# Splitting one feed-forward block of three tiles into one of one tile and one of two

## The chip, the cores and the metric

The kernel runs on one core of a Trainium2 chip. The metric is the device time of one execution in microseconds. TensorE (PE) does the matrix products and transposes, its weight loads (PEld) overlap them; VectorE (DVE) selects the largest scores, ScalarE (ACT) does activations and copies out of PSUM, GpSimd (POOL) does small element-wise work, and SyncE (SP) issues the transfers.

## The reference

Top-32 attention over 8 batches, 8 heads, 576 queries and keys, head dimension 64, followed by a feed-forward layer with an ELU on the 4608 rows that come out. Everything is float32; the weights arrive as float64.

```
scores = scale * np.matmul(q, k.transpose(0, 1, 3, 2))
kth = np.partition(scores, -top_k, axis=-1)[..., -top_k:-top_k + 1]
mask = scores >= kth
scores = np.where(mask, scores, -1000000000.0)
scores = scores - np.max(scores, axis=-1, keepdims=True)
attn = np.exp(scores)
attn = attn / (np.sum(attn, axis=-1, keepdims=True) + 1e-09)
return np.matmul(attn, v).astype(np.float32)
...
x = np.ascontiguousarray(attn_out.transpose(0, 2, 1, 3)).reshape(B * S, H * D)
...
h = x @ w_in
g = np.where(h > 0.0, h, alpha * (np.exp(np.minimum(h, 0.0)) - 1.0))
return (g @ w_out).astype(np.float32)
```

## The kernel before

**Tiles and steps.** A batch's 576 queries are four tiles of 128 and one tile of the last 64 (`J` = 4 names that one). A step is one tile and one pair of heads; the 64 remaining queries take four heads at once, so they need two steps where a full tile needs four. A batch has 18 steps, the kernel 144, numbered through: batch b starts at step 18 b. In even batches the order is tiles 0 and 1, then 2 and 3, then the remainder; in odd batches the remainder comes first (line 606). So the remainders of an even batch and of the odd one behind it are neighbours: steps 52 and 53 of batch 2, 54 and 55 of batch 3.

**One turn of the loop.** The loop of line 681 writes out the order of all four compute engines by hand; each engine runs its own list in that order. Turn n issues, from the top: the scores of step n+2 on PE (L329) and their copies out of PSUM on ACT (L337); the attention products of a finished group (L448) with their copy into `xT` (L475); the selection of step n on DVE, four rounds of `max` (L349, L363) with `match_replace` (L356) between them; the mask of step n-1 on ACT (L385, L386) with a difference on POOL (L384); the transposes of step n-2 on PE (L422) and their copies into `et` on ACT (L423); and the normalising of step n-1 on POOL (L396 to L403). For batches 1 to 7 DVE also transposes k and q of a coming head pair (L283), some turns ahead of the batch; the keys lie in five buffers, so the second head pair of a coming batch takes the buffer that the first pair of the present batch gives back after its last scores.

**Feed-forward blocks.** Rows of x are gathered in blocks. A block of one, two or three tiles becomes ready when the last attention product of its tiles is copied. It then gives 16 hidden pieces and 4 projection pieces for each of its tiles (lines 565 to 575). A hidden piece (L523) is four float32 products of w_in against all columns of the block: 128 columns for one tile, 256 for two, 384 for three. In the trace each product is two MATMUL records and two weight loads, so a hidden piece is 8 records. Behind it ACT takes the relu twice, the exponential and a copy (L533 to L542), for 4, 2 or 2 hidden pieces together, and POOL adds the gate (L493). A projection piece (L551) is four products of 512 columns, again 8 records, and the last of a tile is copied out and stored (L560, L563).

**The pacing.** Pieces are not issued as soon as they could be. `feed` (line 639) runs four times in a turn and spreads them. It knows for each block a ready time in steps and the work of all blocks before it (`due`, lines 618 to 620), in costs of its own: 1.1, 1.85 and 2.7 for a hidden piece of one, two and three tiles, 3.55 for a projection piece. It releases work at the highest constant rate at which the queue does not run empty before any later block's ready time:

```
        ahead = [(w - fed["sum"]) / (x - fed["at"]) for x, w in due if x > fed["at"]]
        if ahead:
            fed["over"] += max(0.0, share * min(ahead))
```

What is left in the queue when the turns are over runs at the end (line 714). The first pair of batches has seven blocks, the other three pairs four each: tiles 0 and 1; tiles 2 and 3; the remainder of both batches together with tiles 0 and 1 of the odd batch; tiles 2 and 3 of the odd batch (line 585).

Of the kernel before, what the change touches and what calls it, by code (L numbers as in the profile page):

```python
# [80 lines left out]
def kernel(  # L81
# [498 lines left out]
    for b in range(B):  # L580
        if b % 2 == 0:
            rest = 2 * J
            division = [(0,), (1,), (2,), (3,), (rest,), (4, 5), (6, 7)]
            if b > 0:
                division = [(0, 1), (2, 3), (rest, 4, 5), (6, 7)]
            slots = {}
            for part in division:
                blk = Block(len(blocks), len(part))
                blocks.append(blk)
                slots.update((x, (blk, s)) for s, x in enumerate(part))  # L590
        first[b] = len(steps)
        tiles = []
        for qt in range(J + 1):
            r0 = b * S + (JP if qt == J else qt if b == 0 else qt * P)
            if qt == J:
                (blk, slot), c0, n = slots[rest], (b % 2) * R, R
                rows = slice(r0, r0 + R)
            else:
                (blk, slot), c0, n = slots[(b % 2) * J + qt], 0, P
                rows = slice(r0, r0 + J * (P - 1) + 1, J) if b == 0 else slice(r0, r0 + P)  # L600
            c0 += slot * P
            t = Tile(b, qt, rows, blk, slice(c0, c0 + n))
            blk.left += NHP
            blk.tiles[slot].append(t)
            tiles.append(t)
        order = [(0, 1), (2, 3), (J,)] if b % 2 == 0 else [(J,), (0, 1), (2, 3)]
        if b == 0:
            order[:2] = [(0,), (1,), (2,), (3,)]
        for qts in order:
            for hp in range(NHP // 2 if qts == (J,) else NHP):  # L610
                group = Group([tiles[qt] for qt in qts], hp)
                steps += [Step(tiles[qt], hp, group, i) for i, qt in enumerate(qts)]
            for qt in qts:
                n = len(steps)
                tiles[qt].block.ready = n + 2.0 if n <= tight else n + 2.5
# [64 lines left out]
    main, rest, other = slice(0, J), slice(J, J + 1), slice(J + 1, 2 * J + 1)  # L680
# [69 lines left out]
```

## Time and profile before

| what | value |
|---|---|
| device time, median of 3 runs | 1633.7 us (1631.86 to 1633.74) |
| profiled execution: device time, span of its instructions | 1633.17 us, 1631.4 us |
| busy: PE, PEld | 1569.5 us (96%), 1004.7 us (62%) |
| busy: DVE, ACT, POOL | 1454.4 us (89%), 1174.6 us (72%), 711.6 us (44%) |
| hidden products L523 | 2432 records, 542.9 us |
| projection products L551 | 1152 records, 522.5 us |
| DVE's MAX8 L363 | 864, mean 751 ns |
| mean granted TensorE clock | 0.988 |
| transfers | 56.17 MB, mean 34 GB/s |

Busy times of PE are unions of records whose ends are modelled, so a stretch in which PE is "busy" may still hold short waits; the distance from one record's start to the next is the better price of a piece. DVE's last instruction for the selection lies more than 100 us before the end of the span: the end is feed-forward work on PE alone.

### The profile page before, as it was taken

What the parts mean: (1) busy time and instruction counts of PE and PEld (TensorE: products, weight loads), DVE (VectorE), ACT (ScalarE), POOL (GpSimd) and SP (SyncE); (2) the same over time, 40 slices, a digit from 0 to 9 for tenths busy, and PEclk for the clock granted to TensorE, in tenths of its full rate; (3) what the DMA queues carried; (4) which work ended last, traced back from release to release, by engine and by line L of the source; (5) the groups of instructions that cost most, each with busy time, mean ns of one, the idle gap of its engine ahead of it and who ended that gap; (6) DMA issues with size and microseconds to landing.
All of it is one profiled execution on the core that took longest, in us unless ns stands there. A gap on an engine that the chain in (4) does not pass through costs nothing.

```text
span 1631.4 us, 25301 instructions
## 1 busy us (share of the span) xinstructions
PE 1569.5 (96%) x8276; PEld 1004.7 (62%) x8276; DVE 1454.4 (89%) x2980; ACT 1174.6 (72%) x2369; POOL 711.6 (44%) x1535
## 2 busy tenths in 40 slices
PE   4789999999999999999999999999999999999999
PEld 2477666766665757555566666655557575755564
DVE  7899999999999999999999699999999599998000
ACT  6987777877776868778577786868668695958521
POOL 4983345444443444444344443535435353534300
PEclk9779999999999999999999999999999999999999
DMA  8521310012100310022000200012100201000000
GB/s 243 187 79 36 65 37 1 7 22 45 43 1 19 54 37 7 7 40 46 23 8 15 55 21 25 1 28 45 36 14 1 43 1 36 1 13 1 7 14 13
DMA packets 188035, 56.17 MB, mean 34 GB/s; under 512 B 178176, under 2 KB 179200, under 8 KB 187904
## 3 DMA queue, kind: packets, MB, share of 16 engines
q1 hardware_dynamic: 186704, 54.26, 14.1%
q8 instruction: 66, 1.08, 0.3%
q14 instruction: 65, 0.53, 0.1%
q10 hardware_dynamic: 1200, 0.30, 0.1%
HBM read 45.09 MB, written 9.44 MB: 33 GB/s over the span
## 4 chain that ended last, share of the span: by engine, by line
PE 74%; ACT 14%; DVE 5%; POOL 3%; issue 1%; SPq 1%; DMA 1%; ACTq 0%; DVEq 0%; POOLq 0%
PE ops L551 29%; PE hps L523 22%; PE avps L448 10%; PE scps L329 7%; PE eps L422 5%; ACT sc L386 3%; DVE wk L356 2%; ACT sc L385 2%; ACT et L423 2%; DVE m L363 2%; ACT n L542 1%; ACT n L533 1%; ACT n L538 1%; ACT gT L536 1%; POOL sc L403 1%
## 5 line engine op out<-in xcount | busy, mean ns | idle before, releaser
L363 DVE MAX8 m<-wk 128x8 f32<-128x576 f32 x864 | 611.2, 751 | 0.3 <-POOL den L384 0.3
L523 PE MATMUL hps<-xT,w_in 128*128 128x256 f32 (+2 forms) x2432 | 542.9, 373 | 0.0
L551 PE MATMUL ops<-w_out,gT 128*128 128x512 f32 x1152 | 522.5, 598 | 0.0
L523 PEld LDWEIGHTS hps<-xT,w_in 128*128 128x128 f32 x2432 | 404.9, 192 | 97.4 <-issue 25.4
L356 DVE MATCH_REPLACE8 wk<-m,wk 128x576 f32<-128x576 f32 x576 | 424.5, 747 | 0.0
L551 PEld LDWEIGHTS ops<-w_out,gT 128*128 128x128 f32 x1152 | 208.6, 190 | 231.7 <-issue 230.6
L396 POOL TENSOR_SCALAR dene<-den 128x2 f32<-128x2 f32 x144 | 32.5, 225 | 693.1 <-ACT sc L386 692.5
L386 ACT ACTIVATE sc<-sc,den 128x576 f32<-128x576 f32 x288 | 223.4, 776 | 66.1 <-POOL den L384 44.4
L385 ACT ACTIVATE sc<-sc,m 128x576 f32<-128x576 f32 x288 | 225.0, 781 | 9.6 <-DVE m L363 9.5
L337 ACT ACTIVATE sc<-scps 128x576 f32<-128x576 f32 x288 | 170.9, 646 | 77.8 <-PE scps L329 77.8
L448 PE MATMUL avps<-et,vT 128*64 128x256 f32 (+2 forms) x2080 | 205.6, 328 | 20.1 <-ACT et L423 19.7
L329 PE MATMUL scps<-kqT 64*128 64x288 f32 (+1 forms) x1280 | 199.9, 443 | 25.1 <-ACT kqT L305 12.6
L349 DVE MAX8 m<-sc 128x8 f32<-128x576 f32 x288 | 202.6, 747 | 20.6 <-ACT sc L337 20.6
L403 POOL TENSOR_SCALAR sc<-sc,rec 128x576 f32<-128x576 f32 x288 | 213.5, 751 | 14.9
L423 ACT COPY et<-eps 128x512 f32<-128x512 f32 x288 | 164.6, 571 | 66.2 <-PE eps L422 66.2
L356 DVE MATCH_REPLACE8 wk<-m,sc 128x576 f32<-128x576 f32 x288 | 212.2, 746 | 0.0
L448 PEld LDWEIGHTS avps<-et,vT 128*64 128x64 f32 x2080 | 128.0, 141 | 101.0 <-ACT et L423 34.2
L422 PEld LDWEIGHTS eps<-ident,sc 128*128 128x128 f32 x1152 | 143.4, 143 | 72.4 <-issue 53.9
L493 POOL TENSOR_TENSOR gT<-n,gT 128x512 f32<-128x512 f32 (+1 forms) x120 | 166.2, 1385 | 38.0 <-ACT n L542 38.0
L422 PE MATMUL eps<-ident,sc 128*128 128x128 f32 x1152 | 174.1, 277 | 0.1
L329 PEld LDWEIGHTS scps<-kqT 64*128 64x128 f32 (+1 forms) x1280 | 107.0, 182 | 102.5 <-issue 46.2
L533 ACT ACTIVATE n<-hps 128x512 f32<-128x512 f32 (+1 forms) x156 | 87.0, 558 | 58.0 <-PE hps L523 57.1
(45 smaller groups left out, 988.5 us busy)
## 6 DMA issues: line engine op xcount, KB each, us to landing
raw<-in_moe_w_in_dram SPq DMA_DIRECT2D x16, 512.0 KB, 4.9
vT<-in_v_dram SPq DMA_DIRECT2D x64, 128.0 KB, 2.4
raw<-in_moe_w_out_dram SPq DMA_DIRECT2D x16, 512.0 KB, 3.8
out_dram<-osb SPq DMA_DIRECT2D x32, 256.0 KB, 2.0
kin<-in_k_dram SPq DMA_DIRECT2D x112, 72.0 KB, 2.4
qin<-in_q_dram SPq DMA_DIRECT2D x112, 72.0 KB, 2.5
kin<-in_k_dram SPq DMA_DIRECT2D x8, 128.0 KB, 4.7
vT<-in_v_dram SPq DMA_DIRECT2D x64, 16.0 KB, 2.2
```

The source lines that it names most:

```text
L329: nc.tensor.matmul(wide[i][rows, half, 0:HS], kq[part, q0 : q0 + u.t.ql], kq[part, k0 : k0 + HS], start=True, stop=True,)
L349: nc.vector.max(found[i], cur[i])
L356: nc.vector.match_replace(wk[i], found[i], cur[i], TAKEN)
L363: nc.vector.max(found[i], cur[i])
L385: nc.scalar.activation(sc, sc, AF.Prelu, scale=-1.0, bias=low, alpha=1.0 / STEEP)
L386: nc.scalar.activation(sc, sc, AF.Exp, scale=-STEEP, bias=gap, accum_out=u.den[:, i : i + 1])
L403: nc.gpsimd.tensor_scalar(u.sc[:, i, :], u.sc[:, i, :], rec[:, i : i + 1], 1.0, ALU.mult, ALU.mult)
L422: nc.tensor.transpose(ps[:, c * P : (c + 1) * P], sc[:, c0 : c0 + P], ident[:])
L423: nc.scalar.copy(g.et[:, chunks, u.at, :], ps[:, 0 : n * P].rearrange("p (c q) -> p c q", c=n),)
L448: nc.tensor.matmul(ps[i * D : (i + 1) * D, cols], vt[:, 2 * J + i if c == J else i * J + c, :], w, start=(c == 0), stop=(c == J),)
L523: nc.tensor.matmul(blk.h[:, f % bank, :], w_in[:, i, f * P : (f + 1) * P], blk.xT[:, i, 0:n_tok], start=(i == 0), stop=(i == NC - 1),)
L551: nc.tensor.matmul(blk.o[:], blk.gT[f // NG][:, f % NG, s * P : (s + 1) * P], w_out[:, f, :], start=(f == 0), stop=(f == NF - 1),)
```

## The change

In the second pair of batches (b == 2) the block of three tiles, the remainder with tiles 0 and 1 of batch 3, becomes a block of one tile (the remainder of both batches) and, behind it, a block of two (tiles 0 and 1 of batch 3). The third and fourth pairs keep four blocks, the first its seven. The first two blocks of the pair, written again in the diff, stay what they were.

```
         if b % 2 == 0:
             rest = 2 * J
             division = [(0,), (1,), (2,), (3,), (rest,), (4, 5), (6, 7)]
-            if b > 0:
+            if b == 2:
+                division = [(0, 1), (2, 3), (rest,), (4, 5), (6, 7)]
+            elif b > 2:
                 division = [(0, 1), (2, 3), (rest, 4, 5), (6, 7)]
```

The block's ready time, its hidden pieces and its column range follow from the division by the lines above, and `due` has one entry more, so `feed` paces other turns differently too. There are 16 hidden pieces more in the program, 2560 records of L523 where there were 2432; projections, attention and transfers of input keep their number.

## The prediction

> **What bounds the kernel now.** I read the strip of 40 slices first, then the chain of waits by engine.
>
> ```profile
> PE   4789999999999999999999999999999999999999
> DVE  7899999999999999999999699999999599998000
> ...
> PE 74%; ACT 14%; DVE 5%; POOL 3%; issue 1%; SPq 1%; DMA 1%; ACTq 0%; DVEq 0%; POOLq 0%
> ```
>
> Two engines are full at once, and DVE stops in the last slices while PE goes on. So the end is set by PE: its total work, plus every moment in which it waits. Less work or fewer waits on PE shorten the kernel; DVE matters only where it makes PE wait.
>
> Where does PE wait? I cut the span into stretches of equal attention work: turns 30 to 65, 66 to 101 and 102 to 137. Each is 36 turns and has the same step types in the same order. A turn begins on PE with its scores; counting the L329 records in PE's timeline puts turns 30, 66, 102 and 138 at 329.78, 698.09, 1078.49 and 1457.92 us. The stretch view gives, per stretch, its length and then PE, PEld, DVE, ACT and POOL busy with record counts; below it the same for L523 alone, then L551 alone.
>
> ```profile
> 329.78:698.09 368.31, 360.03 (x1893) 232.57 (x1892) 365.64 (x753) 273.67 (x551) 161.93 (x374) 1.00 0.13 26
> 698.09:1078.49 380.40, 378.79 (x1926) 235.61 (x1925) 363.85 (x750) 282.43 (x570) 164.94 (x372) 1.00 0.13 26
> 1078.49:1457.92 379.43, 378.12 (x1926) 235.01 (x1925) 358.14 (x737) 281.88 (x569) 164.99 (x373) 1.00 0.10 22
> ...
> 329.78:698.09 368.31, 121.05 (x512) 93.22 (x512) 1.00 0.13 26
> 698.09:1078.49 380.40, 134.28 (x512) 93.32 (x512) 1.00 0.13 26
> ...
> 329.78:698.09 368.31, 116.75 (x257) 46.34 (x256) 1.00 0.13 26
> 698.09:1078.49 380.40, 131.31 (x288) 51.83 (x288) 1.00 0.13 26
> ```
>
> The first stretch has 32 projection records fewer than the second, and its 512 hidden records are all of 256 columns, while 128 in the second are of 384. Yet it is only 12 us shorter. The prices come from PE's timeline, as distances from the start of a group to the start of the next:
>
> ```profile
> 254.71 2.94 PE L523 MATMUL hps<-xT,w_in 128*128 128x128 f32 x24
> 257.50 0.60 PE L422 MATMUL eps<-ident,sc 128*128 128x128 f32 x4
> ...
> 458.36 3.72 PE L523 MATMUL hps<-xT,w_in 128*128 128x256 f32 x16
> 461.91 0.60 PE L422 MATMUL eps<-ident,sc 128*128 128x128 f32 x4
> ...
> 1486.14 8.01 PE L523 MATMUL hps<-xT,w_in 128*128 128x384 f32 x24
> 1493.99 0.60 PE L422 MATMUL eps<-ident,sc 128*128 128x128 f32 x4
> ```
>
> Eight records to a piece: one tile 2.79/3 = 0.93 us, two tiles 3.55/2 = 1.78 (a lone piece, 447.44 to 449.17, took 1.73; I use 1.75), three tiles 7.85/3 = 2.62 (lone: 2.58; I use 2.60). A projection piece is 3.43 us (8 records from 492.24 to 495.68).
>
> So the second stretch holds 4 projections more (13.7 us) and 16 hidden pieces of three tiles for 16 of two (16 x 0.85 = 13.6 us). At its pace the first would take 380.4 - 27.3 = 353.1 us. It took 368.3: 15.2 us are lost to waiting. The waits of PE in the first two stretches name the place:
>
> ```profile
> PE avps L448 <- ACT et L423: 6.4, 9, 2.4
> ...
> PE avps L448 <- ACT et L423: 1.1, 1, 1.1
> ...
> 454.70 3.72 PE L448 MATMUL avps<-et,vT 128*64 128x256 f32 x18 [2.44 <-ACT et L423]
> ```
>
> Attention products wait for ACT's copies of the transposes, nine times against once. Those copies stand behind the masks in ACT's list, and the masks behind DVE's selection. DVE takes 9.64 us for a turn without a key transpose (first MAX8 of one turn to that of the next, 305.10 to 314.74), nearly 10 with them; PE with 6.5 us of pieces by the planner's costs is a little quicker and runs into DVE's results. The listed waits are 6.4 of the 15.2 us; the rest is in PE records that the view counts as busy, and in a slower clock: behind that 2.44 us wait the granted clock is 0.57 from 454 to 458 us, and the 18 records take 3.72 us where 18 of the same took 2.37 (from 477.42). Turns 42 to 45 (449.70 to 496.21, 46.5 us) alone lost 8.7: turns 78 to 81 took 41.65 with 3.8 us more pieces.
>
> **The change, part by part.** *Pacing.* I ran the arithmetic of `feed` for both divisions. Before, the three-tile block is due at 66.5, and no work behind 391.0 counts until then: from turn 30 (155.4 released) the rate is (391.0 - 155.4)/36.5 = 6.45 a turn, afterwards 7.2. Now the one-tile block is due at 58.5 and the next at 66.5 with 422.8 before it, which allows 8.3 and 7.3; the tightest point is 654.8 at 102.5: (654.8 - 155.4)/72.5 = 6.89 from turn 30 to turn 101. So early turns get more pieces, later ones fewer. In pieces: turns 30 to 65 release 11 one-tile hidden pieces and one projection more, 11 x 0.93 + 3.43 = 13.7 us of PE. Turns 66 to 101 release 5 one-tile and 64 two-tile pieces and 35 projections, for 48 two-tile, 16 three-tile and 36: 4.65 + 28.0 - 41.6 - 3.4 = -12.4 us. From turn 102 on both release the same, but for one hidden piece (1.7 us) that slides behind the loop.
>
> *Narrower products.* The two sums differ by +1.3 us, which is the whole cost on PE: 16 x (0.93 + 1.75 - 2.60). Bounds: a one-tile piece cost 0.895 us in a run of two (258.04 to 259.83) and 0.99 alone (250.31 to 251.30): +0.7 to +2.2 us. The Trainium skill, "TensorE: Matmul & The Clock Gate", section "Part 3: Packing small matmuls — row/col tiling", says a weight load overlaps running products only if it uses other row groups, and gives columns/1.2 ns for a load. That speaks against the split: I estimate by it 128 more loads of 128 columns, none hidden, 13.7 us, and a time near 1636. The rows above disagree: 24 narrow records with 24 loads took 2.79 us, 116 ns apart, though the loads' own records last 192 ns.
>
> *ACT, POOL, DVE, SP.* The 40 activations of the three-tile block (L533 to L538) become 36 on the same number of elements, and 8 gates become 12; ACT is busy 273.67 of 368.31 us and POOL 161.93, so both hide it. If ACT's cover were gone, a group of four activations (451.94 to 454.08, 2.1 us) would stand ahead of a copy into `et`, which is the wait shown above. DVE gets nothing. SP issues the same stores and loads, some in other places of its list; transfers use 13% of the engines.
>
> *The waits.* With 13.7 us more work in the first stretch PE is no longer early. DVE needs 357.7 us for turns 30 to 65 (334.02 to 694.42 between their first MAX8, less its own 2.67 us of waiting); PE 353.1 + 13.7 = 366.8. So PE becomes the slower from turn 30 on, as it is from turn 66 on now. It starts about 4 us ahead of DVE's turn (329.78 against 334.02) and gains no more lead, so some waits stay until its lead is worn off. Unknown r: at least 0, at most 10 us (the 8.7 us of turns 42 to 45 come again elsewhere, and a little). I take 4: turns 31 to 37, where DVE has four pairs of transposes and gives PE no lead to lose. A second unknown s: in the second stretch PE waits 1.1 us at L448 and 0.6 at L422, both in turns with three-tile pieces; 0 to 1.7 goes, I take 0.8.
>
> *What is late next.* PE arrives at turn 66 at 329.8 + 366.8 + 4 = 700.6 us, 2.5 later than now with 13.7 us more done, and at turn 102 at 700.6 + 380.4 - 12.4 - 0.8 = 1067.8, 10.7 earlier. What DVE loses in return is free: it already stands still for PE's scores at the key transposes,
>
> ```profile
> 537.51 0.78 DVE L283 STREAM_TRANSPOSE kqT<-kin 128x576 f32<-128x576 f32 x1 [2.67 <-PE scps L329]
> ...
> 911.77 0.78 DVE L283 STREAM_TRANSPOSE kqT<-kin 128x576 f32<-128x576 f32 x1 [16.55 <-PE scps L329]
> ```
>
> and PE does not starve behind the second stop. The 16.55 us shrink, the stop at turn 122 ties DVE to PE again, and everything behind it moves forward as a whole. Sum: 15.2 - 4 + 0.8 - 1.3 = 10.7 us less, 1633.2 - 10.7 = 1622.5 for the profiled execution, which lies 0.5 below the median; I let that stand.
>
> **Rivals.** *A. The waits come again.* Attention products also wait for ACT in turns where PE is late (turn 60, 0.96 us), so the masks' place in ACT's list may cause them whatever the lead. Then r = 10, s = 0, narrow pieces at 2.2: 15.2 - 10 - 2.2 = 3.0 less, 1630.2. Against it: at 7.2 a turn only one such wait in 36 turns.
>
> *B. Slower: narrow products don't hide their loads while PE is full.* The 0.93 us come from turns in which PE had slack. If each narrow record took its own 275 ns instead of 116, 128 x 0.159 = 20.4 us would come on top: 1642.9. It decides from 14 us on, 110 ns more for each record. Against it: in stretches without waits the wide pieces keep their spacing next to full loads, and the narrow ones were back to back.
>
> *C. All of it goes.* r = 0, s = 1.7, narrow at 0.7: 16.2 less, 1617.0. That the division isn't realised can be left out: the changed program has 2560 records of L523.
>
> **How the numbers follow.** Forecast 0.60 (1617 to 1628), A 0.20 (1628 to 1634), B 0.09, C or a little beyond 0.11. Likeliest: 1622.5. The range 1615 to 1632 holds the forecast, C and most of A. What a measurement can tell from no change is 0.2%, 3.3 us, about 1630.4 to 1637. Faster: forecast, C and half of A, 0.81; same: half of A, 0.10; slower: B, 0.09.
>
> **What would show it.** In the changed profile, turns 30 to 65 should take about 371 us with 600 hidden and 264 projection records, their waits at L448 should fall from 6.4 to 2 or 3 us, and no drop of the clock near 455. Turns 66 to 101 should take 367, and turns 102 to 137 again 379. The stop of 16.55 us should be shorter, and that of turn 122 (16.91 us) as long as it is. Narrow pieces in a row should stand 0.9 to 1.0 us apart. I am wrong if the first stretch takes over 377 us (the waits stayed), or narrow pieces over 1.5 us (B).

## The result, and the profile after

The changed kernel takes 1637.51 us (median of 11 runs, 1635.51 to 1638.94) against 1633.71 us (11 runs, 1631.86 to 1635.07): ratio 1.0023, interval 1.0014 to 1.0033. It is slower, by 3.8 us. The profiled execution is the quickest of the eleven (1635.51 us, span 1633.7), so the trace shows 2.3 us of the 3.8.

The strip and the chain after:

```profile
PE   4789999999999999999999999999999999999999
DVE  6899999999999899999999699999999599998100
```

```profile
PE 74%; ACT 15%; DVE 5%; POOL 5%; issue 1%; DMA 0%; SPq 0%; ACTq 0%; DVEq 0%; POOLq 0%
```

PE still sets the end. Its turns 30, 66, 102 and 138 now begin at 330.78, 705.90, 1082.49 and 1463.31 us. The stretches of 36 turns between them (length; PE, PEld, DVE, ACT, POOL busy and records), then L523 and L551 alone in the first:

```profile
330.78:705.90 375.12, 367.91 (x1989) 242.26 (x1989) 368.72 (x761) 277.68 (x559) 161.41 (x372) 1.00 0.13 26
705.90:1082.49 376.59, 370.99 (x1957) 240.61 (x1956) 362.10 (x743) 279.63 (x564) 165.69 (x378) 1.00 0.13 25
1082.49:1463.31 380.82, 379.12 (x1926) 234.24 (x1925) 356.01 (x734) 280.84 (x568) 165.03 (x373) 1.00 0.10 22
...
330.78:705.90 375.12, 131.78 (x600) 103.91 (x600) 1.00 0.13 26
...
330.78:705.90 375.12, 120.39 (x264) 47.56 (x264) 1.00 0.13 26
```

PE's longest wait in the first stretch and in the second, by the view of waits (us in total, times, longest):

```profile
PE avps L448 <- ACT et L423: 6.1, 5, 3.0
...
PE avps L448 <- ACT et L423: 5.2, 6, 1.5
```

The pieces moved forward as worked out: 600 hidden and 264 projection records in the first stretch. It grew by 6.8 us for 13.7 us more work, so about 6.9 us of lost time went, though the listed waits at L448 fell only from 6.4 to 6.1 us. But the second stretch, relieved of 12.4 us of work, became only 3.8 us shorter: 8.6 us were lost there, and waits at L448 that it hardly had (1.1 us) are now 5.2 us, 4.1 of the 8.6.

Where the waits sit is seen turn by turn. At turn 57 PE stands still for 3.04 us (PE's timeline first, then ACT's; start, length, instruction):

```profile
613.08 0.33 PE L448 MATMUL avps<-et,vT 128*64 128x64 f32 x2
616.45 2.40 PE L448 MATMUL avps<-et,vT 128*64 128x64 f32 x38 [3.04 <-ACT et L423]
...
612.91 0.78 ACT L386 ACTIVATE sc<-sc,den 128x576 f32<-128x576 f32 x1 [0.37 <-ACT sc L385]
613.59 0.19 ACT L386 ACTIVATION_READ_ACCUMULATOR sc<-sc,den 128x1 f32 x1
613.68 0.57 ACT L533 ACTIVATE n<-hps 128x512 f32<-128x512 f32 x1
614.16 0.58 ACT L536 ACTIVATE gT<-hps 128x512 f32<-128x512 f32 x1
614.64 0.63 ACT L538 ACTIVATE n<-n 128x512 f32<-128x512 f32 x1
615.29 0.63 ACT L542 ACTIVATE n<-n 128x512 f32<-128x512 f32 x1
615.83 0.57 ACT L423 COPY et<-eps 128x512 f32<-128x512 f32 x1
```

PE waits for the copy at 615.83. Between the mask and that copy ACT works through the four activations of a hidden pair, 2.15 us that no one is in a hurry for. They stand there because the pair ended in the third of the turn's four releases, which comes right before the last transposes and their copy. I call this the bad place: a hidden unit (a pair, or four narrow pieces) that ends in the third quarter of a turn, with attention products in the next turn, right behind its scores. From the released pieces, turns 28 to 145 have 7 bad places before (attention products at turns 28, 32, 42, 50, 60, 72, 108) and 10 after (28, 34, 42, 52, 57, 78, 88, 96, 98, 106). Before has none from turn 73 to 107, the change has five, and three of these (88, 96, 98) show waits of 1.54, 1.22 and 1.52 us. Not every bad place costs a wait: PE has none at turns 72 and 108 before, and none at 52, 78 and 106 after.

### The profile page after: what moved, and what is told of

The parts are those of the page before. It is cut to its first block, busy times and chain, and to the rows that moved or that the text cites. A ratio compares the mean times of both kernels' runs of the same rounds, so it can differ in the third digit from the quotient of the medians.

```text
span 1633.7 us, 25562 instructions
## 1 busy us (share of the span) xinstructions
PE 1567.3 (96%) x8404; PEld 1016.4 (62%) x8404; DVE 1453.9 (89%) x2980; ACT 1174.6 (72%) x2369; POOL 712.0 (44%) x1539
## 4 chain that ended last, share of the span: by engine, by line
PE 74%; ACT 15%; DVE 5%; POOL 5%; issue 1%; DMA 0%; SPq 0%; ACTq 0%; DVEq 0%; POOLq 0%
PE ops L551 29%; PE hps L523 21%; PE avps L448 10%; PE scps L329 8%; PE eps L422 5%; ACT sc L386 3%; ACT sc L385 2%; DVE wk L356 2%; ACT et L423 2%; DVE m L363 2%; ACT n L542 2%; ACT n L533 1%; ACT n L538 1%; ACT gT L536 1%; POOL sc L403 1%
## 5 line engine op out<-in xcount | busy, mean ns | idle before, releaser
L523 PE MATMUL hps<-xT,w_in 128*128 128x256 f32 (+2 forms) x2560 | 545.2, 363 | 0.0
L551 PE MATMUL ops<-w_out,gT 128*128 128x512 f32 x1152 | 522.9, 598 | 0.0
L523 PEld LDWEIGHTS hps<-xT,w_in 128*128 128x128 f32 x2560 | 420.5, 192 | 86.1 <-issue 23.7
L551 PEld LDWEIGHTS ops<-w_out,gT 128*128 128x128 f32 x1152 | 208.4, 190 | 230.9 <-issue 228.9
L448 PE MATMUL avps<-et,vT 128*64 128x256 f32 (+2 forms) x2080 | 202.4, 328 | 23.4 <-ACT et L423 23.4
L329 PE MATMUL scps<-kqT 64*128 64x288 f32 (+1 forms) x1280 | 198.6, 441 | 25.7 <-ACT et L423 12.5
L448 PEld LDWEIGHTS avps<-et,vT 128*64 128x64 f32 x2080 | 125.3, 142 | 104.9 <-ACT et L423 36.7
```

The costliest lines, as they stand in the source:

```text
L329: nc.tensor.matmul(wide[i][rows, half, 0:HS], kq[part, q0 : q0 + u.t.ql], kq[part, k0 : k0 + HS], start=True, stop=True,)
L448: nc.tensor.matmul(ps[i * D : (i + 1) * D, cols], vt[:, 2 * J + i if c == J else i * J + c, :], w, start=(c == 0), stop=(c == J),)
L523: nc.tensor.matmul(blk.h[:, f % bank, :], w_in[:, i, f * P : (f + 1) * P], blk.xT[:, i, 0:n_tok], start=(i == 0), stop=(i == NC - 1),)
L551: nc.tensor.matmul(blk.o[:], blk.gT[f // NG][:, f % NG, s * P : (s + 1) * P], w_out[:, f, :], start=(f == 0), stop=(f == NF - 1),)
```

## The experiments

Three theories. **Place**: the bad place costs the time, whatever the division. **Lead**, that of the prediction: PE waits where it runs ahead of DVE. **Narrow**: the one-tile block itself costs it. Runs of before beside the experiments had medians from 1632.88 to 1633.77 us.

**e1: the old division, moved to bad places.** In turn 73 the release account loses 1.8 of the planner's units once, so that from turn 74 on pieces fall one or two quarters later.

```
         place[0] += 1
+        if place[0] == 4 * 73 + 1:
+            fed["over"] += -1.8
         close_gates(2 if n > tight + 3 else 6)
```

> The kernel before, with 1.8 planner units taken from the release account once, in turn 73; the division, the pacing and the products are those of before, and all turns up to 72 are issued as before. From turn 74 on the pieces fall one or two quarters of a turn later, so that seven pairs of two-tile hidden pieces end in the third quarter of a turn whose next turn begins with attention products (turns 80, 82, 88, 90, 91, 96, 98), where before had none. Place theory: each costs PE 1 to 2 us at L448; turns 66 to 101 take 387 to 392 us instead of 380, and the span is 1638 to 1643. Lead theory (PE waits only when it runs ahead of DVE, the one of the prediction): turns 66 to 101 stay at 380 and the span at 1631 to 1633. Narrow theory (the one-tile block itself costs): the same as the lead theory, 1631 to 1633.

Median 1643.53 us, ratio 1.0062 (1.0047 to 1.0077), span 1641.1. The first two stretches:

```profile
329.76:698.41 368.65, 360.29 (x1894) 232.61 (x1893) 365.68 (x753) 273.83 (x551) 162.52 (x375) 1.00 0.13 26
698.41:1088.57 390.16, 380.96 (x1925) 234.86 (x1924) 370.34 (x763) 283.44 (x570) 166.03 (x372) 1.00 0.13 26
```

The first stretch is that of before; the second grew by 9.8 us with the same work and no new block, and its L448 waits from 1.1 to 8.7 us. Neither lead nor narrow gives this: both left the stretch at 380 us.

**e2: the new division at the old pace.**

```
-        due.append((blk.ready, total))
+        if blk.number != 9:
+            due.append((blk.ready, total - (31.8 if blk.number == 10 else 0.0)))
```

> The changed division, paced as before: the one-tile block has no due time of its own and 391.0 is due at 66.5 again, so turns up to 65 are issued as in before. Place theory: turns 30 to 65 take the 368 us of before with the same wait of 2.4 us near turn 42; behind turn 66 eight pairs end badly (turns 80, 88, 90, 96, 98, 106, 118, 127), turns 66 to 101 lose 7 to 10 us, the span is 1639 to 1643. Lead theory: turns 30 to 65 as before, 66 to 101 without new waits, span 1632 to 1634. Narrow theory: the loss of the change is there with either pacing, span 1633 to 1636, with no L448 waits in turns 73 to 101.

Median 1645.38 us, ratio 1.0074 (1.0057 to 1.0091), span 1642.7. The first stretch took 368.7 us with the L448 waits of before (6.4 us); the second 389.4 us, with 8.0 us of waits instead of 1.1. So the new pace was not what made the change slow, it even made it less so. The listed waits at L448 are 6.9 of the 9.0 us by which the second stretch is longer than before; only one of the seven, 0.8 us at turn 68, stands behind narrow pieces.

**e3 and e4: no unit may end in the third quarter**, in the changed kernel and in the one before. Pieces carry a flag that is true where a unit ends.

```
         while ffn and decoded[0] >= ffn[0][1] and 0.5 * ffn[0][0] <= fed["over"]:
+            if n > 24 and place[0] % 4 == 3 and ffn[0][4]:
+                break
```

> The changed kernel, with one rule more in the release loop: from turn 25 on a hidden piece that ends its pair (or four) isn't released in the third quarter of a turn, but in the fourth. Place theory: the L448 waits at turns 34, 42, 57, 88, 96 and 98 go; turns 30 to 65 lose about 8 us, turns 66 to 101 about 8; span 1617 to 1624. Lead theory: the waits come from PE's lead on DVE and stay within 3 us of the changed kernel's, span 1630 to 1636. Narrow theory: 1631 to 1636.

> The kernel before with the same rule as in the run before this one. Place theory: the waits at turns 32, 42, 50 and 60 go, turns 30 to 65 take 358 to 362 us instead of 368, the rest is unchanged within 3 us, span 1621 to 1626. Lead theory: PE still runs ahead of DVE in turns 30 to 65, waits stay, span 1629 to 1634. Narrow theory: no narrow block, no change, 1629 to 1634.

e3: median 1623.75 us, ratio 0.9941 (0.9926 to 0.9955), span 1621.0; stretches 370.5, 369.8 and 380.1 us; waits at L448 in the first two 2.0 and 0.9 us. e4: 1624.28 us, ratio 0.9944 (0.9929 to 0.9958), span 1622.3; 363.0, 380.1 and 379.0 us; waits 2.3 and 1.4 us. Both spans are where the place theory put them; e4's first stretch is 1 us over its range. In e3 the first two stretches became 4.6 and 6.8 us shorter than in the changed kernel, where about 8 us each were expected.

The rule moves pieces on PE too, so it could have helped by giving PE something to do in the fourth quarter (the cover theory). **e5 and e6** leave PE's list alone and change only ACT's: the activations of a piece in the third quarter are kept back until the copy is issued.

```
+            later.append(lambda a=(blk.gT[f // NG], f % NG + 1, blk.n, blk.h): behind(*a))
+            if place[0] % 4 != 3 or place[0] < 100 or place[0] > 4 * NS:
+                settle_acts()
...
         if done:
             turn(done, other)
+        settle_acts()
```

Here `behind` holds the four activations and the gate's entry in its list; a projection piece calls `settle_acts()` before it starts.

> The changed kernel with the lists of PE, DVE and POOL left word for word as they are; on ACT alone, 24 copies into et move ahead of the activation group (relu, relu, exponential, copy) that a hidden pair ending in the third quarter of a turn puts before them. Place theory, in the form that ACT's order is the cause: the L448 waits at turns 34, 42, 88, 96 and 98 go and that at 57 falls from 3.0 to under 1 us; turns 30 to 65 take 366 to 370 us instead of 375, turns 66 to 101 370 to 372 instead of 377; span 1618 to 1625. Cover theory (PE waits because nothing stands in the fourth quarter to work on meanwhile, and holding pieces back helped by filling it): PE's list is the same, so the waits stay, at 57 above all; span 1630 to 1635.

> The same edit in the kernel before: 19 copies move ahead of an activation group, nothing else. Place theory by ACT's order: the waits at turns 32, 42, 50 and 60 go, turns 30 to 65 take 359 to 364 us instead of 368, the rest stays; span 1621 to 1627. Cover theory: the wait of 2.4 us at turn 42 stays, span 1629 to 1632.

e5: median 1620.38 us, ratio 0.9918 (0.9902 to 0.9935), span 1619.1; stretches 368.5, 370.1 and 379.7 us. e6: 1622.55 us, ratio 0.9933 (0.9919 to 0.9948), span 1621.3; 362.9, 379.3 and 377.9 us. Turn 57 in e5, PE and then ACT:

```profile
609.06 0.33 PE L448 MATMUL avps<-et,vT 128*64 128x64 f32 x2
610.27 1.38 PE L448 MATMUL avps<-et,vT 128*64 128x64 f32 x38 [0.89 <-ACT et L423]
...
609.57 0.19 ACT L386 ACTIVATION_READ_ACCUMULATOR sc<-sc,den 128x1 f32 x1
609.66 0.56 ACT L423 COPY et<-eps 128x512 f32<-128x512 f32 x1
610.12 0.60 ACT L538 ACTIVATE n<-hps 128x512 f32<-128x512 f32 x1
610.61 0.60 ACT L541 ACTIVATE gT<-hps 128x512 f32<-128x512 f32 x1
```

The copy comes right after the mask, the activations behind it, and the wait falls from 3.04 to 0.89 us, with the same PE list. The cover theory falls; the cause is ACT's order.

With the order mended on both sides, the split is worth something: 1620.38 (1619.42 to 1620.93) against 1622.55 us (1622.06 to 1623.11), four runs each that do not overlap.

**e7 and e9: the split in all later pairs, with ACT's order mended and not.**

```
-            if b == 2:
-                division = [(0, 1), (2, 3), (rest,), (4, 5), (6, 7)]
-            elif b > 2:
-                division = [(0, 1), (2, 3), (rest, 4, 5), (6, 7)]
+            if b >= 2:
+                division = [(0, 1), (2, 3), (rest,), (4, 5), (6, 7)]
```

> The kernel of the run e5_split_copyfirst with the division into five blocks in the third and fourth pairs of batches too. 22 hidden units (pairs or fours) end in the third quarter ahead of attention products, against 10; if ACT's order is the cause and is mended, that costs nothing now. Each further split costs 1.3 us on PE (16 x (0.93 + 1.75 - 2.60)) and ends the waits of 1 to 2 us that the three-tile pieces bring at turns 104 to 107. Place theory: span 1617 to 1622, L448 waits no more than in that run. If the place still costs 1 to 1.5 us a time by itself, span 1632 to 1638.

> The changed kernel with five blocks in the third and fourth pairs too, and ACT's order as it was: the run e7_all_split without its copies moved ahead. PE's list is that run's. 22 hidden units end in the third quarter ahead of attention products; 19 of them two-tile pairs. Place theory: at 1 to 2 us each the span is 1624 to 1640, at least 14 us over e7_all_split, and the L448 waits of PE rise above 25 us. If the gain of that run came from the division alone and not from ACT's order, 1608 to 1612.

e7: median 1608.65 us, ratio 0.9849 (0.9832 to 0.9865), span 1608.0, the quickest of all. e9: 1648.79 us, ratio 1.0101 (1.0083 to 1.0119), span 1645.5. The longest wait of e9 in the view of PE's waits, and the first three of e7:

```profile
PE avps L448 <- ACT et L423: 37.6, 33, 2.7
```

```profile
PE scps L329 <- ACT et L423: 13.3, 6, 3.3
PE scps L329 <- ACT kqT L305: 12.3, 4, 8.4
PE avps L448 <- ACT et L423: 11.9, 13, 2.1
```

The two differ in ACT's order alone: 40 us, of which the listed waits at L448 are 25.7. e9's span is 5.5 us above what I expected at most, e7's 9 us below its range: I had not counted that other small losses go. Priced by the turn, with attention and pieces at what they take in turns without waits, I estimate that PE loses 3.2, 0.8 and 0.0 us in e7's three stretches and 7.3, 7.6 and 4.6 us in e5's. What makes the losses of e5 that e7 does not have, ACT's order elsewhere or PSUM, was not found. e7's stretches take 375.9, 377.0 and 379.6 us, 14.2 us more than e5's together, but from turn 138 on it takes 144.7 us where e5 takes 170.4: fewer pieces are left there (136 projection records instead of 168), and its hidden pieces are narrower.

**e8: the copies of the second quarter ahead of its activations too.** The test of e5 becomes `place[0] % 4 not in (2, 3)`, with `settle_acts()` also behind `turn(done, rest)`.

> The kernel of the run e5_split_copyfirst, where the activation groups of pairs that end in the second quarter also stand behind the copies of that quarter (main and rest) on ACT. Attention products don't wait for those, so the place theory expects little: span 1617 to 1620. If the remaining excess of about 1 us in turns 44, 70, 80 and 90 comes from this order, 1614 to 1617; if late hidden activations hold the PSUM buffers and so the next hidden products, 1621 to 1626.

Median 1625.46 us, ratio 0.9951 (0.9936 to 0.9966), span 1622.3: 5.1 us slower than e5. The small losses it was to test did not go (1.15 us at turn 44, 1.17 at 70, 1.60 at 80 and 1.12 at 90). The span fits late hidden activations that hold the PSUM buffers, but no run showed that this is what happened.

| kernel | bad places | stretches 30, 66, 102 (us) | waits L448 in the first two (us) | span (us) |
|---|---|---|---|---|
| before | 7 | 368.3, 380.4, 379.4 | 6.4, 1.1 | 1631.4 |
| after | 10 | 375.1, 376.6, 380.8 | 6.1, 5.2 | 1633.7 |
| e1, old division shifted | 16 | 368.7, 390.2, 381.4 | 6.4, 8.7 | 1641.1 |
| e2, split at old pace | 14 | 368.7, 389.4, 384.6 | 6.4, 8.0 | 1642.7 |
| e3, split held | 0 | 370.5, 369.8, 380.1 | 2.0, 0.9 | 1621.0 |
| e4, before held | 0 | 363.0, 380.1, 379.0 | 2.3, 1.4 | 1622.3 |
| e5, split, copy first | 10, order mended | 368.5, 370.1, 379.7 | 1.5, 0.9 | 1619.1 |
| e6, before, copy first | 7, order mended | 362.9, 379.3, 377.9 | 2.2, 0.3 | 1621.3 |

## Why the prediction was wrong

**The bound** was right: in every run PE is at 90% or more in all slices behind the third, and DVE stops before it.

**Pacing** was right to the record: 600 and 264 records in the first stretch, and one hidden piece more behind the loop.

**Narrower products** were right. In turn 65 of the changed kernel:

```profile
699.36 2.94 PE L523 MATMUL hps<-xT,w_in 128*128 128x128 f32 x24
702.14 0.60 PE L422 MATMUL eps<-ident,sc 128*128 128x128 f32 x4
```

24 records in 2.78 us, 0.93 us a piece, now where PE is full; all 16 narrow pieces took 14.8 us, from 0.89 to 0.99 us each. Rival B falls, and with it the estimate from the Trainium skill ("TensorE: Matmul & The Clock Gate", "Part 3"; its price of a load stands in "Part 2"): the loads are hidden here.

**The waits in the first stretch**: 15.2 us were there, I left r = 4 of them; 375.1 - 353.1 - 13.7 = 8.3 us stayed, inside the bounds of 0 to 10, but not for the reason given. With ACT's order mended, e5's 368.5 us leave 1.7, so 6.6 of the 8.3 are that order, which the prediction did not count; that r stayed inside its bounds is luck. The signs set for this stretch failed: the listed waits at L448 did not fall to 2 or 3 us, and the drop of the clock went from 455 us but came at 616 us instead. And of the 15.2 us that I put down to PE's lead, ACT's order makes 5.4 (368.3 us before, 362.9 in e6).

**The step that failed** is the term s of "The waits", which let waits behind turn 66 go (0 to 1.7 us) and put new ones at nothing, and with it "What is late next", which moved everything forward as a whole. They let the second stretch take 380.4 - 12.4 - 0.8 = 367.2 us; it took 376.6, so instead of 0.8 us gained 8.6 us were lost. Of these, 6.5 go when ACT's order alone is mended (e5's 370.1 us): PE waited for copies that stood behind hidden activations in ACT's list. The other 2.1 stay open. PE should have been at turn 66 at 700.6 and at turn 102 at 1067.8 us; it came at 705.9 and 1082.5. So of the 14.7 us by which it was late, 5.3 arose up to turn 66 (1.0 of it before turn 30) and 9.4 in the second stretch. Turns 102 to 137 added 1.4 (380.8 for 379.4), the end gave 3.0 back (170.4 us from turn 138 for 173.5): 13.0 us over the predicted span of 1620.7. The step rested on a reading: that PE waits for ACT's copies because it is ahead of DVE, so that a later PE finds the copies made. The trace of the change speaks against it: PE began turns 96 and 98 5.0 and 8.5 us after DVE had begun them, and waited 1.22 and 1.52 us all the same. I saw that the copies stand behind the masks in ACT's list, and costed the activation group ahead of a copy as a loss only "if ACT's cover were gone". ACT had idle time, but a list in order has no use for it: what counts is what stands ahead of the copy. And I counted the pieces that `feed` releases in 36 turns, not the quarter in which they end. The old rate of 7.2 a turn from turn 73 to 107 happened to end every two-tile pair in an even quarter (four hidden pieces or two projections a turn); 6.89 drifts through the quarters. That four of nine waits in the first stretch stood at bad places (28 lies ahead of it: 32, 42, 50, 60) could have been read off the trace of before.

**Rivals.** A named the mechanism, "the masks' place in ACT's list may cause them whatever the lead", but with s = 0 it too held that no new waits come behind turn 66; its 1630.2 was too low for the same reason. What stood against it, one such wait in 36 turns at 7.2 a turn, was a chance of phase. C, that all waits go, did not come; even with ACT's order mended e5's 1620.38 us lie above its 1617.0.

**What of the lead theory stands.** With ACT's order mended, e5's first stretch is 5.6 us longer than e6's for 13.7 us more work, so 8.1 us of waiting go with the pace, of the 11.2 I had claimed. In e6's first stretch the view of waits shows none of DVE, and PE begins 33 of the 36 turns ahead of it, in e5's 17: there DVE sets PE's pace, so the mechanism is real and smaller. The second stretch is 9.2 us shorter for 12.4 us less work, which gives 3.2 back; why is open. So is what gave 3.0 us back behind turn 138.

## What to carry to other kernels

Before moving work between the turns of a loop that is written out by hand, list for each engine what lands ahead of what, in the finest unit in which the loop releases work; an engine with a quarter of its time idle can still stop another one by order alone. The copy or the mask that the bounding engine waits for belongs ahead of work that has slack. A change that looks like one of size or balance may be judged by a chance of phase, so mend the order first: here the split in all pairs is 16 us slower than the division before with one order of ACT (e9 against before), and 14 us quicker with the other (e7 against e6).

## What the hardware showed

The TensorE clock can fall at a short wait. In the kernel before, the granted clock was 0.57 from 454 to 458 us around a wait of 2.44 us; in the changed one 0.76 from 614 to 618 us around the wait of 3.04 us, and the 38 attention records behind it took 2.40 us where e5, without that wait, needed 1.38. So such a wait can cost about 1 us more than the view of waits says. Not every one does: behind e9's wait of 2.69 us at turn 141 the clock stayed at 1.00, and 18 records took 2.37 us that took 3.72 behind the wait of 2.44 us. The changed kernel, then e9 (PE's timeline and the stretch behind it):

```profile
614.00:618.00 4.00, 1.55 (x29) 1.55 (x30) 4.00 (x9) 3.46 (x7) 3.34 (x11) 0.76 0.00 0
...
1541.93 2.37 PE L448 MATMUL avps<-et,vT 128*64 128x256 f32 x18 [2.69 <-ACT et L423]
...
1542.00:1546.00 4.00, 4.00 (x26) 2.85 (x27) 0.44 (x1) 0.37 (x1) 2.31 (x5) 1.00 0.00 0
```

The Trainium skill, "TensorE: Matmul & The Clock Gate", section "Part 1: The HAM clock gate", lets the clock fall after an idle window of about 3.4 us; the waits of 2.44 and 3.04 us were shorter, and the measurement decides. What makes one short wait lower the clock and another not, no run here shows.

The same page, in its table of specifications, gives ACT a queue in strict order of eight entries. The runs agree on the order: the copy that PE needs at turn 57, moved ahead of four activations in e5, starts right behind the mask, 2.15 us earlier relative to it. The eight entries no run here shows.
